# Moving the last sums of a frequency group behind the next group's first product in a fused Fourier filter and MLP

## The chip, the cores and the metric

The kernel runs on one core of a Trainium2 chip. The metric is the device time of one launch in microseconds. Names used below: TensorE (PE in the profile) multiplies matrices into PSUM; VectorE (DVE), ScalarE (ACT) and GpSimd (POOL) work elementwise; SyncE (SP) issues most transfers. Each engine takes its instructions in the order in which the program issues them, and waits where an operand is not ready.

## The reference

Two parts follow each other. A global Fourier filter along the sequence, and then a two-layer MLP whose activation is h - tanh(h):

```python
# batch 8, sequence 3008, channels 256, 1505 frequencies, d_ff 2048, all float32
X = np.fft.rfft(x, axis=1)
Y = X * (filt_r + 1j * filt_i)[None]
y = np.fft.irfft(Y, n=3008, axis=1)
t = y.reshape(8 * 3008, 256)
h = t @ w_in
out = (h - np.tanh(h)) @ w_out
```

## The kernel before

**Stages.** 3008 = 64 x 47, so the transform is made of matrix products. For each batch element b there are four stages. *First* (`first`): 12 steps of products of length 64, whose results go to a DRAM scratch tensor `ct1`. *Middle* (`middle`): products of length 47 forth, the multiplication with the filter, and products back, over seven groups of frequencies, from `ct1` to a second scratch tensor `ct2`. *Last* (`last`): products of length 64 back, from `ct2` into SBUF as the tokens of the MLP, in six chunks of four sequence rows. *MLP* (`up`, `shrink`, `down`): for every chunk, four quarters of d_ff.

**The loop.** The main loop runs over U, 4 quarters of 48 groups (8 elements b times 6 chunks c), 192 in all. At U it issues `up` of quarter U, `shrink` of U - 1 and `down` of U - 2, interleaved by hand inside `up` (L493 to L551). In `up` there are five slots, the calls `t(0)` to `t(4)`. A place in the loop is written (c, u, k) here: chunk, quarter, slot; its position in an element is 20c + 5u + k, from 0 to 119. While element p passes the MLP, the slots carry the middle stage of element p + 1 and the first stage of element p + 2 (for element 0, those of 1, and the first stages of 1 and 2). Element 7 has neither beside it.

**The order.** `planned` (L947) gives every step of these stages a due position: the 12 first steps and the 58 middle steps are each spread evenly from 0.2 to LAG (in element 0 the middle from LEAD = 30). `t(k)` (L994) takes the first step of the sorted list if its due position has come, one step for one slot. Slots 0 and 2 of quarter u = 3 are kept for `last` of the next chunk. A step is whatever a generator does up to its next `yield`.

**A middle group.** For group g of seven (six of 120 rows and one of 48) the steps are, with the names used below:

- F1: issue the loads of group g + 1 (`a2` from `ct1`, `ft`, the filter); two products (L327) into a PSUM bank, and ACT's copy to `xy` (L330).
- F2: two products (L327), and DVE's sum and difference with F1's result into `xy` (L332, L333).
- M1: POOL multiplies `xy` by the filter's real part into `nn` (L342, one buffer). M2: POOL multiplies `xy` by the imaginary part in place (L345).
- M3: POOL's two sums into `nn` (L347, L348).
- S: DVE's last sum and difference from `nn` into `xy` (L350, L351).
- B1 and B2: two products each (L361) from `xy`, ACT's copy (L364) and the write to `ct2` from ACT's queue.

`xy`, `a2`, `ft` and the copies `e1` have two buffers each. In the kernel before a group runs F1, F2, M1, M2, then B1 and B2 of the group before, M3, S.

**Banks.** The products of the slots go to a PSUM bank that `zd` chooses (L909): in slots 1, 2 and 3 it is bank `y` if the one before was `t`, otherwise `t`. Bank `y` is also the target of the second product of `up` in each quarter, which DVE reads at L509. So a product that a slot puts into `y` has to wait for L509 of its quarter. Bank `x` is freed for the next quarter by DVE's L534, bank `z` is read at L526 and L542.

**What DVE does in a quarter,** in program order: slot 0, L509, L564 (it waits for ACT's arctangent and square, L557 and L560), slot 1, L571 (it waits for ACT's square L568), slot 2, L526, L564, L534, slot 3, L571, slot 4, L542. (In element 0 slot 1 comes after the next product, and slot 3 before the last x product and L534.) Where u is 1, the sums of `down` come between (L632, L638, L643, L644, L650), and where u is 2 two transposes at slot 2 (L671). POOL forms four sums of the activations after the second L571 (`combine`, L466 to L469 on `t`), and four of the tokens after `last` (the same lines on `tu`).

Of the kernel before, what the change touches and what calls it, by code (L numbers as in the profile page):

```python
# [28 lines left out]
SLOTS = [(a, min(SG, NA - a)) for a in range(0, NA, SG)]  # L29
# [4 lines left out]
FACTORS = [(0.28138768672943115, 0.18210311233997345, 0.5012423992156982),  # L34
           (0.28138768672943115, -0.6558710336685181, 0.19358105957508087)]

LEAD, LAG = 30, 102

S, K = 0.6389930153911744, 0.3476472316053873
A, B = 0.18659689165196622, -0.6846325776203513  # L40
# [51 lines left out]
def kernel(  # L92
# [32 lines left out]
    def ways(g, back):  # L125

        if g < len(SLOTS) - 1:
            m = [mats[0:KM, (3 * back + k) * KM:(3 * back + k + 1) * KM] for k in range(3)]
            return m[0], m[0], m[1], m[2]
        at = 6 * KM + 4 * back * KL  # L130
        return [mats[0:KL, at + k * KL:at + (k + 1) * KL] for k in range(4)]
# [168 lines left out]
    def rows(t, b, g, first_block=0, n=4):  # L300

        a, s = SLOTS[g]
        return dram(t[b], (first_block * NA + a) * NH * DM,
                    [[DM, s * NH], [NA * NH * DM, n], [1, DM]])

    def load_a2(b, g, tag="a2", bufs=2):

        n = SLOTS[g][1] * NH
        t = tr.tile([KM, 4, DM], F32, tag=tag, bufs=bufs, name="a2")
        nc.sync.dma_start(t[0:n], rows(ct1, b, g))  # L310
        return t

    def load_ft(g):
        n = SLOTS[g][1] * NH
        t = tr.tile([KM, 4, DM], F32, tag="ft", bufs=2, name="ft")
        nc.sync.dma_start(t[0:n], dram(filt_d, g * KM * 4 * DM, [[4 * DM, n], [1, 4 * DM]]))
        return t

    def forth(g, at, z):

        n = SLOTS[g][1] * NH
        xy = tr.tile([KM, 4, DM], F32, tag="xy", bufs=2, name="xy")[0:n]
        way = ways(g, 0)
        for v in (1, 0):
            pa = z("pa", [128, 2, DM])[0:n]
            for k in range(2):
                nc.tensor.matmul(pa[:, k], way[2 * v + k], at[0:n, 2 * v + k],  # L327
                                 start=True, stop=True)
            if v:
                ACT.copy(xy[:, 2:4], pa)  # L330
                yield xy
        V.tensor_add(xy[:, 0:2], pa, xy[:, 2:4])  # L332
        V.tensor_sub(xy[:, 2:4], pa, xy[:, 2:4])  # L333
        yield

    def filtered(g, xy, ft, by, by2):

        n = SLOTS[g][1] * NH
        ab = xy.rearrange("p (x v) c -> p x v c", v=2)
        fv = ft[0:n].rearrange("p (x v) c -> p x v c", v=2)  # L340
        nn = tr.tile([KM, 4, DM], F32, tag="nn", bufs=1, name="nn")[0:n]
        by.tensor_mul(nn.rearrange("p (x v) c -> p x v c", v=2), ab,  # L342
                      fv[:, :, 0:1].to_broadcast([n, 2, 2, DM]))
        yield
        by.tensor_mul(ab, ab, fv[:, :, 1:2].to_broadcast([n, 2, 2, DM]))  # L345
        yield
        by2.tensor_sub(nn[:, 0:4:3], nn[:, 0:4:3], xy[:, 1:3])  # L347
        by2.tensor_add(nn[:, 1:3], nn[:, 1:3], xy[:, 0:4:3])  # L348
        yield
        V.tensor_add(xy[:, 0:2], nn[:, 0:2], nn[:, 2:4])  # L350
        V.tensor_sub(xy[:, 2:4], nn[:, 0:2], nn[:, 2:4])  # L351
        yield

    def back(b, g, xy, z):

        n = SLOTS[g][1] * NH
        way = ways(g, 1)
        for v in range(2):
            pe = z("pe", [128, 2, DM])[0:n]
            for k in range(2):  # L360
                nc.tensor.matmul(pe[:, k], way[2 * v + k], xy[:, 2 * v + k],  # L361
                                 start=True, stop=True)
            e1 = tr.tile([KM, 2, DM], F32, tag="e1", bufs=2, name="e1")[0:n]
            ACT.copy(e1, pe)  # L364
            ACT.dma_start(rows(ct2, b, g, 2 * v, 2), e1)
            yield

    def middle(b, z):

        a2, ft = {0: load_a2(b, 0)}, {0: load_ft(0)}  # L370
        waiting = iter(())
        yield
        for g in range(len(SLOTS)):
            if g + 1 < len(SLOTS):
                a2[g + 1], ft[g + 1] = load_a2(b, g + 1), load_ft(g + 1)
            there = forth(g, a2.pop(g), z)
            xy = next(there)
            yield
            next(there)
            yield  # L380
            done = filtered(g, xy, ft.pop(g), G, G)
            next(done)
            yield
            next(done)
            yield
            for _ in waiting:
                yield
            next(done)
            yield
            if g + 1 == len(SLOTS):  # L390
                yield
            for _ in done:
                yield
            waiting = back(b, g, xy, z)
        yield
        for _ in waiting:
            yield

    def filter_rows(g):

        a, s = SLOTS[g]
        for v, src in enumerate((filt_r.tensor, filt_i.tensor)):
            if g < len(SLOTS) - 1:
                yield v, 0, NH * s, dram(src, (a + 1) * DM, [[NQ * DM, NH], [DM, s], [1, DM]])
                for m, n in ((1, 16), (17, 7)):
                    yield 2 + v, m * s, n * s, dram(src, (NQ * m - a - 1) * DM,
                                                    [[NQ * DM, n], [-DM, s], [1, DM]])
            else:
                yield v, 0, NH, dram(src, (a + 1) * DM, [[NQ * DM, NH], [1, DM]])
                yield v, NH, NH, dram(src, 0, [[NQ * DM, NH], [1, DM]])  # L410
                for m, n in ((1, 16), (17, 7)):
                    yield 2 + v, m, n, dram(src, (NQ * m - a - 1) * DM, [[NQ * DM, n], [1, DM]])
# [377 lines left out]
    with tc.tile_pool(name="tr", bufs=2) as tr, tc.manual_schedule():  # L790
        with tc.tile_pool(name="pro", bufs=1) as pro, \
# [79 lines left out]
            waiting = iter(())  # L871
            last_g = len(SLOTS) - 1
            for g in range(last_g + 1):
# [3 lines left out]
                xy = next(there)  # L877
# [3 lines left out]
                done = filtered(g, xy, fts.pop(g), V, G)  # L881
# [5 lines left out]
                waiting = back(0, g, xy, z0)  # L887
# [16 lines left out]
        with tc.tile_pool(name="dn", bufs=2) as dn, \  # L904
# [42 lines left out]
            def planned(p):  # L947

                def spread(n, lo, hi, *what):
                    return [(lo + (hi - lo) * k / n, *what, k) for k in range(n)]  # L950

                n_m = 8 * len(SLOTS) + 2
                f = [spread(NX, *((0.2, LEAD / 2) if b == 1 else (LEAD / 2, LEAD) if b == 2
                                  else (0.2, LAG)), firsts, b, first)
                     for b in ([1, 2] if p == 0 else [p + 2]) if b < BATCH]
                m = [spread(n_m, LEAD if p == 0 else 0.2, LAG, mids, b, middle)
                     for b in [p + 1] if b < BATCH]
                return sorted(sum(f + m, []), key=lambda s: s[0])

            firsts, mids = {1: fs}, {}  # L960
            for U in range(total + 2):
                i, u = divmod(U, 4)
                if U < total:
                    p, c = groups[i]
                    if c == 0 and u == 0:
                        steps = planned(p)
                    if u == 0 and i + 1 < len(groups) and c + 1 < NC:
                        e2s[i + 1] = load_e2(*groups[i + 1])
                    if u == 2 and i + 1 < len(groups) and c + 1 == NC:
                        assert not steps  # L970
                        e2s[i + 1] = load_e2(*groups[i + 1])
                    if u == 1 and c + 1 == NC:
                        for gens, ahead, what in ((mids, 2, middle), (firsts, 3, first)):
                            if p + ahead < BATCH:
                                gens[p + ahead] = what(p + ahead, z1)
                                next(gens[p + ahead])
                    if u == 2 and i + 1 < len(groups):
                        lasts = last(i + 1, z1)
# [91 lines left out]
```

## Time and profile before

| | us |
|---|---|
| median of three runs | 2903.82 (2903.04 to 2906.41) |
| the profiled execution | 2905.42 |
| its span | 2903.6 |
| TensorE busy | 2730.1 (94%) |
| VectorE busy | 2067.3 (71%) |
| GpSimd busy | 1897.8 (65%) |
| ScalarE busy | 1762.8 (61%) |
| mean granted TensorE clock | 0.977 |

Busy time of TensorE is the union of matrix instructions with modelled ends, so it also counts time at a lower clock. One product of 128 x 128 by 128 x 256 leaves two records; four records start 0.86 us apart from the next four when nothing waits. The first 145 us prepare the weights and the first element's transforms; the loop over U begins there. The waits in the profile are named by what came last: "PE pa L327 <- DVE h L509" is a product of F1 or F2 that waited for DVE's reading of bank y.

### The profile page before, as it was taken

The numbers are of one execution on the slowest core, as the hardware profiler recorded it, in microseconds if no ns is written. First come the engines' busy times: TensorE is split into PE (matmuls) and PEld (weight loads), VectorE is DVE, ScalarE is ACT, GpSimd is POOL, SyncE is SP. The second block draws the span as 40 slices with busy tenths as digits, with TensorE's granted clock in tenths as the row PEclk, the third lists the DMA queues.
The fourth block names the chain that finished last, engine by engine and source line by source line (L and its number), as shares of the span: only waits on it lengthen the run. The fifth ranks groups of instructions, "written<-read, shape, count | busy, mean of one in ns | idle before, by whom it ended". The sixth has DMA issues, their size and how long they took to land.

```text
span 2903.6 us, 36938 instructions
## 1 busy us (share of the span) xinstructions
PE 2730.1 (94%) x12830; PEld 2376.1 (82%) x12830; DVE 2067.3 (71%) x2283; ACT 1762.8 (61%) x2583; POOL 1897.8 (65%) x1391
## 2 busy tenths in 40 slices
PE   4499999999999999999999999999999999999998
PEld 3388888888888888898888888888888888799886
DVE  4777777777677767777677766767767777677776
ACT  2156566566665666566665666656666566566665
POOL 4557886767657776666666766576675777655553
PEclk7699999999999999999999999999999999999999
DMA  9474223223232332233223331232323122101010
GB/s 244 133 227 126 63 49 86 76 63 80 66 73 68 84 85 60 64 77 95 55 60 69 98 84 49 55 99 73 78 50 71 47 57 58 28 20 36 19 26 17
DMA packets 341639, 215.48 MB, mean 74 GB/s; under 512 B 227736, under 2 KB 300988, under 8 KB 341251
## 3 DMA queue, kind: packets, MB, share of 16 engines
q1 hardware_dynamic: 296851, 154.15, 22.7%
q10 hardware_dynamic: 39504, 50.61, 5.6%
q0 software_dynamic: 5088, 8.28, 1.1%
q8 instruction: 103, 1.69, 0.3%
q14 instruction: 93, 0.76, 0.1%
HBM read 137.83 MB, written 78.12 MB: 74 GB/s over the span
## 4 chain that ended last, share of the span: by engine, by line
PE 65%; DVE 13%; POOL 11%; issue 4%; ACT 3%; DMA 2%; SPq 0%; ACTq 0%; DVEq 0%; POOLq 0%
PE o L618 26%; PE x L486 17%; PE z L486 8%; PE y L486 4%; DVE h L564 4%; PE pu L452 3%; PE pe L361 3%; DVE h L571 2%; PE pa L327 2%; PE pf L295 2%; POOL nn L347 2%; POOL nn L348 2%; ACT y L560 2%; POOL t L469 2%; DVE xy L351 1%
## 5 line engine op out<-in xcount | busy, mean ns | idle before, releaser
L564 DVE TENSOR_TENSOR h<-h,y 128x1024 f32<-128x1024 f32 (+1 forms) x384 | 598.1, 1558 | 288.0 <-ACT y L560 287.4
L618 PE MATMUL o<-t,wd 128*128 128x256 f32 (+1 forms) x3072 | 776.0, 375 | 0.0
L571 DVE SCALAR_TENSOR_TENSOR h<-sq,h 128x1024 f32<-128x1024 f32 (+1 forms) x384 | 600.8, 1564 | 123.2 <-ACT sq L568 115.1
L618 PEld LDWEIGHTS o<-t,wd 128*128 128x128 f32 x3072 | 583.6, 190 | 69.6 <-issue 2.4
L466 POOL TENSOR_TENSOR t<-h 128x512 f32<-128x512 f32 (+1 forms) x190 | 240.7, 1267 | 604.1 <-DVE h L571 371.2
L486 PE MATMUL x<-tu,wu 128*128 128x256 f32 (+1 forms) x2304 | 593.4, 381 | 0.0
L618 PE MATMUL o<-h,wd 128*128 128x256 f32 (+1 forms) x2304 | 584.8, 376 | 5.4 <-DVE h L571 5.1
L486 PEld LDWEIGHTS x<-tu,wu 128*128 128x128 f32 x2304 | 439.6, 193 | 58.9 <-issue 5.6
L618 PEld LDWEIGHTS o<-h,wd 128*128 128x128 f32 x2304 | 432.7, 190 | 60.9 <-DVE h L571 11.3
L568 ACT ACTIVATE sq<-y,near_b 128x1024 f32<-128x1024 f32 (+1 forms) x384 | 435.1, 1133 | 25.8 <-DVE h L571 20.1
L557 ACT ACTIVATE y<-h 128x1024 f32<-128x1024 f32 (+1 forms) x384 | 397.4, 1035 | 12.4 <-ACT e L364 7.3
L560 ACT ACTIVATE y<-y 128x1024 f32<-128x1024 f32 (+1 forms) x384 | 399.7, 1041 | 6.5 <-ACT a L296 0.4
L492 ACT COPY s<-x 128x512 f32<-128x512 f32 (+1 forms) x192 | 110.8, 577 | 424.6 <-PE x L486 419.3
L492 ACT COPY u<-x 128x512 f32<-128x512 f32 (+1 forms) x384 | 221.0, 576 | 225.5 <-PE x L486 203.1
L469 POOL TENSOR_TENSOR t<-t,h 128x512 f32<-128x512 f32 (+1 forms) x190 | 351.9, 1852 | 0.0
L467 POOL TENSOR_TENSOR t<-h,t 128x512 f32<-128x512 f32 (+1 forms) x190 | 245.9, 1294 | 14.9
L468 POOL TENSOR_TENSOR t<-h 128x512 f32<-128x512 f32 (+1 forms) x190 | 244.8, 1288 | 0.0
L486 PE MATMUL x<-ut,wu 128*128 128x256 f32 (+1 forms) x768 | 199.7, 382 | 30.6 <-DVE h L534 29.7
L526 DVE TENSOR_TENSOR h<-z,u 128x512 f32<-128x512 f32 (+1 forms) x192 | 128.8, 671 | 104.8 <-ACT u L492 103.7
L486 PE MATMUL z<-tu,wu 128*128 128x256 f32 (+1 forms) x768 | 196.7, 379 | 3.4 <-DVE h L542 3.4
L486 PE MATMUL z<-ut,wu 128*128 128x256 f32 (+1 forms) x768 | 194.4, 375 | 1.1 <-DVE h L526 1.0
L486 PEld LDWEIGHTS x<-ut,wu 128*128 128x128 f32 x768 | 140.0, 189 | 67.7 <-DVE h L534 52.7
(116 smaller groups left out, 3469.5 us busy)
## 6 DMA issues: line engine op xcount, KB each, us to landing
e<-ct SPq DMA_DIRECT2D x48, 512.0 KB, 4.6
a<-ct SPq DMA_DIRECT2D x48, 480.0 KB, 5.0
ct<-e ACTq DMA_DIRECT2D x96, 240.0 KB, 2.6
ct<-a ACTq DMA_DIRECT2D x84, 256.0 KB, 3.0
x_sb<-in_x_dram SPq DMA_DIRECT2D x161, 128.0 KB, 4.2
ft<-filt SPq DMA_DIRECT2D x42, 480.0 KB, 6.6
out_dram<-ot SPq DMA_DIRECT2D x1248, 16.0 KB, 1.5
gt<-g SPq DMA_DIRECT2D x48, 256.0 KB, 3.1
```

What stands on the lines that cost most here:

```text
L466: by.tensor_sub(t[0], b[0][1], b[0][0])
L467: by.tensor_sub(t[1], b[1][1], t[0])
L468: by.tensor_sub(t[2], b[1][1], b[0][1])
L469: by.tensor_sub(t[3], t[1], b[1][0])
L486: nc.tensor.matmul(bank[:, k], wu[:, q - 1, (2 * u + k) * 128:(2 * u + k + 1) * 128], rhs[q - 1], start=(first and k == 0), stop=True, ski ...
L492: ACT.copy(t, X)
L557: ACT.activation(y[k], ht[k], AF.Arctan, scale=S)
L560: ACT.activation(y[k], y[k], AF.Square, accum_out=y_sums[:, 2 * U + k // 2:2 * U + k // 2 + 1])
L564: V.tensor_mul(ht[k], ht[k], y[k])
L568: ACT.activation(sq[k], y[k], AF.Square, bias=near_b, scale=A)
L571: V.scalar_tensor_tensor(out=ht[k], in0=sq[k], scalar=K, in1=ht[k], op0=ALU.add, op1=ALU.mult)
L618: nc.tensor.matmul(product(q), wd[:, q - 1, (2 * u + k) * 128: (2 * u + k + 1) * 128], rhs[q - 1][:, k], start=(u == 0 and k == 0 and q == ...
```

## The change

S of a group moves into the next group, behind that group's F1. F2 and M1 follow; then come B1 of the group before, M2, B2 of the group before, and M3. A group now runs F1, S of the group before, F2, M1, B1 of the group before, M2, B2 of the group before, M3. The number of steps stays 58. At the end of an element there are two empty steps, and then S, B1 and B2 of the seventh group. Before, there was one empty step, S, another empty step, B1 and B2. LAG is 104 in place of 102. `filtered`, `forth`, `back`, `planned` and the slots are as they were.

```diff
-LEAD, LAG = 30, 102
+LEAD, LAG = 30, 104
 ...
-        waiting = iter(())
+        before = None
         yield
         for g in range(len(SLOTS)):
             if g + 1 < len(SLOTS):
                 a2[g + 1], ft[g + 1] = load_a2(b, g + 1), load_ft(g + 1)
             there = forth(g, a2.pop(g), z)
             xy = next(there)
             yield
+            if before:
+                next(before[0])
+                yield
             next(there)
             yield
             done = filtered(g, xy, ft.pop(g), G, G)
             next(done)
             yield
-            next(done)
-            yield
-            for _ in waiting:
+            if before:
+                next(before[1])
                 yield
             next(done)
             yield
-            if g + 1 == len(SLOTS):
+            if before:
+                next(before[1])
                 yield
-            for _ in done:
-                yield
-            waiting = back(b, g, xy, z)
-        yield
-        for _ in waiting:
-            yield
+            next(done)
+            yield
+            before = done, back(b, g, xy, z)
+        yield
+        for k in (0, 1, 1):
+            yield
+            next(before[k])
+        yield
```

## The prediction

> **What bounds the kernel now.** First the page's first part and its chain: TensorE is busy 94% of the span, and 65% of the chain that ended last is its matmuls. But 13% is DVE and 11% POOL, among them the two filter sums on POOL (L347, L348) and a last sum (L351).
>
> ```profile
> PE 2730.1 (94%) x12830; PEld 2376.1 (82%) x12830; DVE 2067.3 (71%) x2283; ACT 1762.8 (61%) x2583; POOL 1897.8 (65%) x1391
> ...
> PE 65%; DVE 13%; POOL 11%; issue 4%; ACT 3%; DMA 2%; SPq 0%; ACTq 0%; DVEq 0%; POOLq 0%
> PE o L618 26%; PE x L486 17%; PE z L486 8%; PE y L486 4%; DVE h L564 4%; PE pu L452 3%; PE pe L361 3%; DVE h L571 2%; PE pa L327 2%; PE pf L295 2%; POOL nn L347 2%; POOL nn L348 2%; ACT y L560 2%; POOL t L469 2%; DVE xy L351 1%
> ```
>
> Next the windows, one for each batch element. Element 2 (of 0 to 7, a middle stage beside it) leaves TensorE 11.1 us idle of 348.2, element 6 12.4 of 341.1, element 7, with no middle stage beside it, 0.6 of 283.8:
>
> ```profile
> 846.90:1195.10 348.20, 337.11 (x1602) 295.12 (x1602) 246.03 (x263) 219.39 (x321) 232.00 (x161) 0.99 0.30 74
> ...
> 2239.90:2581.00 341.10, 328.73 (x1554) 286.59 (x1553) 253.71 (x263) 212.44 (x309) 241.02 (x161) 0.98 0.20 48
> 2581.00:2864.80 283.80, 283.18 (x1369) 252.51 (x1368) 208.37 (x226) 191.18 (x275) 162.47 (x124) 1.00 0.11 24
> ```
>
> The waits name the pair: DVE stands 106.3 us in front of the last sums, and TensorE waits for DVE sums that are queued behind them.
>
> ```profile
> DVE xy L350 <- POOL nn L348: 106.3, 35, 6.6
> ...
> PE pa L327 <- DVE h L509: 40.0, 11, 5.0
> ...
> PE x L486 <- DVE h L534: 29.7, 39, 1.5
> ```
>
> The timeline of element 1 shows how, first DVE, then PE. S.0 sits at slot (0,2,0) (chunk, quarter, slot). It waits for POOL until 529.07; L509, which frees bank y, is behind it; F1.1 at the next slot wants bank y, so TensorE stands from 527.8 to 532.8.
>
> ```profile
> 529.07 1.60 DVE L350 TENSOR_TENSOR xy<-nn 120x512 f32<-120x512 f32 x1 [2.21 <-POOL nn L348]
> 530.60 1.61 DVE L351 TENSOR_TENSOR xy<-nn 120x512 f32<-120x512 f32 x1
> 532.13 0.61 DVE L509 TENSOR_TENSOR h<-y,s 128x448 f32<-128x448 f32 x1
> ```
>
> ```profile
> 526.05 1.78 PE L618 MATMUL o<-h,wd 128*128 128x224 f32 x8
> 532.80 1.84 PE L327 MATMUL pa<-a,mats_sb 120*120 120x256 f32 x4 [4.96 <-DVE h L509]
> ```
>
> Afterwards the granted clock is half (column PEclk, third from the end, 0.50), so the stall of 5.1 costs 6.9:
>
> ```profile
> 533.10:536.40 3.30, 3.30 (x10) 2.77 (x9) 1.05 (x1) 0.82 (x2) 2.73 (x3) 0.50 0.00 0
> ```
>
> The Trainium skill ("TensorE: Matmul & The Clock Gate", Part 1) has the clock fall after an idle window of about 3.4 us. Here it also fell after stalls of 2.65 us (0.50 at 623 to 625 us), so by the page those five stalls would have cost 1.7 us less each; the trace decides.
>
> **What is at stake.** I take the starts of successive y products as the length of a quarter. In element 7 a quarter is 12.09 us (12.41 where u is 1, 13.87 where u is 3, near 11.5 in chunk 0), 24 of them 297.7. A product of four records adds 4 x 0.216 = 0.86. Elements 1 to 5 carry 28 middle and 12 first products more: 297.7 + 40 x 0.86 = 332.2, measured 348.2, so 16.0 lost in each. Where: (0,2) 19.46 against 12.59, 6.9; (2,0) 19.11 against 14.68, 4.4; (3,1) 15.41 against 14.14, 1.3; (4,2) 1.3; (4,0) 1.0; the rest 1.1. Element 6: 341.1 - 321.9 = 19.2, mostly (4,0) 6.7 and (0,2) 5.4. Element 0, by the same differences from (1,3) on: 10.6. In all 10.6 + 5 x 16.0 + 19.2 = 110 us.
>
> **The change, part by part.** Nothing is added to or taken from any engine; instructions move. I laid out both orders on the slots by the rule in the code (one step in each free slot whose place has come; a slot is 348.2 / 120 = 2.9 us).
>
> *LAG 104.* The spacing grows from 101.8 / 58 = 1.755 to 103.8 / 58 = 1.790 slots. The last back product moves from place 100.2 to 102.2; the next element's e2 load stands at 110, over 20 us later, and the write lands in 2.6 us. Cost nothing; without that cover, the load's 4.6 us once per element.
>
> *S one step later, behind F1.* S.0 goes to (0,2,1), F1.1 in front of it. L509 no longer stands behind S, so F1.1 starts at once. By the rows POOL is through at 529.04, and DVE comes to S about 529.6 (the ACT squares ended 527.73; F1's copy 0.59 and L564 1.2 come first), so no wait. The pair costs 3.2 beside POOL's L466 (1.60 and 1.61, against 0.69 alone), leaving L534 0.4 late for bank x and F2's sums 0.6 late for bank y: 1.1 instead of 6.9.
>
> At (2,0) it is not cured: M3.2 falls at (1,3,4), one slot later than now, which puts it behind the four L466 to L469 sums on POOL. Now it runs in front of them:
>
> ```profile
> 614.16 2.25 POOL L348 TENSOR_TENSOR nn<-nn,xy 120x512 f32<-120x512 f32 x1
> 616.37 1.27 POOL L466 TENSOR_TENSOR t<-h 128x512 f32<-128x512 f32 x1
> ```
>
> L571 ends near 615.7, four sums of 1.27 to 1.7 reach 621, M3 2.5 to 4.5 more: 624.5. S.2 at (2,0,1) ends about 626; then end sum 1.2, F2's pair 1.4, L526 0.7, L564 1.2, L534 0.7: 631.2. TensorE wants bank z at 627.9 (L526 ends 629.3) and bank x at 630.2: 1.4 + 1.0 = 2.4, range 0.5 to 5. F2.3 itself on y isn't held, since L509 is ahead of S. Now it costs 4.4.
>
> The other S: at (1,1,1) and (2,3,1) M3 is four and five slots old, no wait; at (3,1,4) and (4,0,3) S stands behind L534 and delays only L542 and L509, which have slack; at (5,0,0) the back product follows at the next slot: TensorE needs 0.86 + 0.86 + 1.73 from bank z's last product, DVE 0.68 + 1.35 + 0.68, taken as 0.5. So (3,1) goes from 1.3 to about 0 with 0.2 at (3,2), (4,0) from 1.0 to 0.2.
>
> The present loss at (3,1): the 3.63 us in front of L350 push L534, which frees bank x:
>
> ```profile
> 699.98 0.69 DVE L350 TENSOR_TENSOR xy<-nn 120x512 f32<-120x512 f32 x1 [3.63 <-POOL nn L348]
> ...
> 705.18 0.68 DVE L534 COPY h<-x 128x512 f32<-128x512 f32 x1
> ```
>
> *Back products behind M1 and M2.* S lies three steps (15 us) ahead of them, no cost. Alternating with steps that use no bank, they mostly get another bank; twice an element (at (0,3), (3,3)) two products in t follow each other over slots 3 and 4, each perhaps 0.3 for ACT's copy (0.58): 0.6. M3.6 goes from slot 2 of (4,2), beside the transposes L671, to slot 4: 1.3 to about 0.6.
>
> *Queues and buffers.* M1 needs the single nn buffer two steps after S instead of three; at (2,0) S ends 626, M1.3 comes after 629: nothing. F1's loads on SP's queue now stand three steps behind M2 of the group before, not five; SP already waits 163.8 us for M2 (20 times), in front of stores of 1.5 us and loads used eight steps (40 us) later, landing in 6.6: nothing. ACT's ct2 writes follow their products; POOL's queue holds no DMA here after 323 us.
>
> *Sum.* Elements 1 to 5: 1.1 at (0,2), 2.4 at (2,0), 0.5 at (5,0), 0.4 for (3,2) and (4,0), 0.6 for bank t, 0.6 at (4,2) and 0.9 of the present rest = 6.5 for 16.0, 5 x -9.5 = -47.5. Element 6: S.0 and S.5 at (0,2,1) and (4,0,3), no late S left but (2,0,0): about 5 for 19.2, -14. Element 0: S.2 and S.4 come to slot 0 with F2 on y at slot 1, but there the sums of L466 on ut are through before; 8 for 10.6, -2.6. Together -64. Against it stands one price that the slots don't settle: the pair of S takes 1.4 on a free DVE, 3.3 beside POOL, now 2.0 in the mean (L350 944 ns, L351 1053). Over 49 moved pairs that is 29 us less to 64 more, and by the 2.7 us that two sums late at L534 cost at (2,1) of element 0 it can reach TensorE in full. I take the middle, +17, as POOL is busy for 65% of the span. So -47.
>
> The Trainium skill ("SBUF — State Buffer", "SBUF: two separate sides") calls that an exclusive lock: a DVE instruction with two SBUF inputs waits out the POOL instruction. The rows agree (L350 ended 0.55 us after POOL's L466 did, at 530.12). Were S to meet M1 or M2 (3.2 us each), the rule would make the pair 6.4, which is 2.9 above what the slower rival takes; no S does so by the slots.
>
> The profiled execution took 2905.42 (span 2903.6); 2905.4 - 47 = 2858. The median of the three runs, 2903.82, is 1.6 below, inside what I can resolve.
>
> **The rivals.** *Half of it (0.18).* Only the big stalls of 5.4 to 6.9 go (5 x 5.8 + 4.5 + 6.3 = 40), and (2,0) gets a cold clock, 5 x 1.7 back: 2874. For it: M3.2 behind the combine. Against: the waits in five other quarters end as surely.
>
> *Everything hidden (0.10).* The full 110 goes: 2796; 80 of it, 2826. For it: DVE is only 71% busy. Against: (2,0).
>
> *Slower: DVE in front of L534 (0.12).* S and F2's sums now stand in neighbouring steps. If both fall ahead of L534 in one quarter, S at its longest row (1.75 each), DVE is 3.5 + 1.4 = 4.9 late, less what it idles there (1.1 in front of L571, 1.0 in front of L526): 2.8 for each of 49 groups against 110 / 49 = 2.2 now, +27: 2932. It decides above 2.2 a group. For it: DVE's idle time is spread and S has no cover of its own. Against: only at (2,0) do both stand there; F2 falls behind L534 in three other groups.
>
> *No change (0.05).* Each wait is paid at the next bank: 2903, within 6 us (0.2%, about what three runs from 2903.0 to 2906.4 can tell).
>
> **How the numbers follow.** Forecast 0.55 with its own range 2838 to 2876 (the residue of 6.5 down to 3 or up to 10 in each element). Faster 0.55 + 0.18 + 0.10 = 0.83, same 0.05, slower 0.12. The range 2826 to 2896 leaves out the slower case, no change, and the far end of the hidden one.
>
> **What would show it.** Right: the wait of pa on L509 from 40 us to under 10; DVE's wait for L348 from 106 to under 40, what is left at (2,0); no half clock after (0,2); elements near 339. Wrong: pa or pe waiting for L350 or L509 at new slots, x waiting for L534 over 40 us, half-clock stretches more than five.

## The result, and the profile after

Median of four runs 2877.05 us (2872.96 to 2878.8), against 2903.66 (2903.04 to 2906.41) for four of the kernel before: ratio 0.9904, 95% interval 0.9887 to 0.9922. The change is faster by 26.6 us where 47 was forecast. The time lies inside the range on record (2826 to 2896) and 1 us outside the forecast's own (2838 to 2876); of the cases, "Half of it" with 2874 came nearest. The profiled execution took 2878.8, its span is 2877.0, the mean granted clock 0.982 (before 0.977).

The page of the kernel after, its first and its fourth part (busy time, and the chain that ended last). From L368 on, line numbers are five higher than before: L514 is the old L509, L539 the old L534.

```profile
PE 2719.1 (95%) x12830; PEld 2361.4 (82%) x12830; DVE 2105.3 (73%) x2283; ACT 1761.2 (61%) x2583; POOL 1927.1 (67%) x1391
...
PE 68%; DVE 17%; POOL 4%; issue 4%; ACT 4%; DMA 3%; SPq 1%; ACTq 0%; DVEq 0%; POOLq 0%
```

POOL's share of the chain fell from 11% to 4%: it is no longer waited for in the old place. DVE's rose from 13% to 17%, and DVE is busy for 38 us more though it executes the same 2283 instructions. The windows of elements 2 and 6 (length, then busy time by engine, clock and DMA) show the gain and its limit: 348.2 became 343.0, and of that TensorE is still idle for 7.8; 341.1 became 334.0.

```profile
847.10:1190.10 343.00, 335.18 (x1602) 292.15 (x1601) 253.44 (x263) 219.23 (x321) 237.67 (x161) 1.00 0.31 75
2219.10:2553.10 334.00, 326.65 (x1554) 284.26 (x1553) 258.24 (x263) 212.32 (x309) 244.43 (x161) 0.99 0.21 49
```

The waits of DVE and of TensorE after (who waits for what: us in total, times, longest):

```profile
DVE xy L350 <- POOL nn L348: 29.4, 16, 4.5
```

```profile
PE x L491 <- DVE h L539: 26.9, 37, 4.1
...
PE pa L327 <- DVE h L514: 10.3, 7, 1.7
...
PE o L623 <- POOL t L473: 6.2, 8, 0.9
...
PE pe L361 <- DVE h L514: 5.0, 5, 1.0
```

DVE's wait in front of the last sums went from 106.3 to 29.4. Seven of the 16 that remain lie ahead of the loop (20.3 us; a kernel below keeps these alone), and only 6.4 of the rest at (2,0). TensorE's wait for the reading of bank y went from 40.0 to 10.3. New are a wait of `o` for POOL's combining, and one of B's products (`pe`) for bank y.

The place that the prediction showed, S.0 of an element (here element 2), first DVE, then TensorE. F1.1 starts at 874.52 with no wait in front of it, S.0 has its operands, and the clock in the stretch that was cold before is full (1.00; before, at 881.40 to 884.70, it was 0.51).

```profile
879.71 1.62 DVE L350 TENSOR_TENSOR xy<-nn 120x512 f32<-120x512 f32 x1
881.25 1.62 DVE L351 TENSOR_TENSOR xy<-nn 120x512 f32<-120x512 f32 x1
```

```profile
874.52 1.03 PE L327 MATMUL pa<-a,mats_sb 120*120 120x256 f32 x4
...
882.37 1.40 PE L623 MATMUL o<-t,wd 128*128 128x224 f32 x6 [0.89 <-POOL t L473]
```

The trace's clock record has 13 stretches at half clock from the loop's start to the end of element 6 before, and 3 after. Two of the three are new, in element 0 and in element 6, both at (2,1). In element 0 S stands 1.59 us for M3 in front of L539, and x behind it for 4.12, so the stall that the change takes from (0,2) has come back there in front of another bank. The last section comes to the one in element 6.

```profile
294.05 0.69 DVE L350 TENSOR_TENSOR xy<-nn 120x512 f32<-120x512 f32 x1 [1.59 <-POOL nn L348]
294.66 1.72 DVE L351 TENSOR_TENSOR xy<-nn 120x512 f32<-120x512 f32 x1
296.31 0.68 DVE L539 COPY h<-x 128x512 f32<-128x512 f32 x1
```

```profile
297.04 2.08 PE L491 MATMUL x<-ut,wu 128*128 128x256 f32 x4 [4.12 <-DVE h L539]
```

Lengths of the elements, from the starts of the y products, in us:

| element | 0 | 1 | 2 | 3 | 4 | 5 | 6 | rest |
|---|---|---|---|---|---|---|---|---|
| before | 353.2 | 348.6 | 348.2 | 348.2 | 348.2 | 348.4 | 341.1 | 322.7 |
| after | 358.6 | 343.0 | 343.0 | 343.0 | 343.0 | 343.0 | 334.0 | 324.0 |

Where the code of an element is unchanged, its length still differs by 2 to 4 us from kernel to kernel (the rest from 320.0 to 324.0), so only larger differences of a single element are read below. In elements 1 to 5 of the kernel after, the same quarter has the same length within 0.1 us. A quarter's length also holds its slots' products, 0.86 us each; where an edit moves one into another quarter, the text says so.

### The profile page after: what moved, and what is told of

The parts are those of the page before. It is cut to its first block, busy times and chain, and to the rows that moved or that the text cites. A ratio compares the mean times of both kernels' runs of the same rounds, so it can differ in the third digit from the quotient of the medians.

```text
span 2877.0 us, 36939 instructions
## 1 busy us (share of the span) xinstructions
PE 2719.1 (95%) x12830; PEld 2361.4 (82%) x12830; DVE 2105.3 (73%) x2283; ACT 1761.2 (61%) x2583; POOL 1927.1 (67%) x1391
## 4 chain that ended last, share of the span: by engine, by line
PE 68%; DVE 17%; POOL 4%; issue 4%; ACT 4%; DMA 3%; SPq 1%; ACTq 0%; DVEq 0%; POOLq 0%
PE o L623 28%; PE x L491 17%; PE z L491 8%; PE y L491 5%; DVE h L569 5%; DVE h L576 3%; PE pu L457 3%; PE pe L361 3%; PE pa L327 2%; PE pf L295 2%; DVE xy L351 2%; ACT y L565 1%; DMA x<-in_x_dram 1%; DVE h L539 1%; POOL nn L348 1%
## 5 line engine op out<-in xcount | busy, mean ns | idle before, releaser
L569 DVE TENSOR_TENSOR h<-h,y 128x1024 f32<-128x1024 f32 (+1 forms) x384 | 604.2, 1574 | 274.4 <-ACT y L565 274.2
L576 DVE SCALAR_TENSOR_TENSOR h<-sq,h 128x1024 f32<-128x1024 f32 (+1 forms) x384 | 614.8, 1601 | 104.3 <-ACT sq L573 95.3
L471 POOL TENSOR_TENSOR t<-h 128x512 f32<-128x512 f32 (+1 forms) x190 | 239.1, 1258 | 587.4 <-DVE h L576 345.6
L491 PE MATMUL x<-tu,wu 128*128 128x256 f32 (+1 forms) x2304 | 583.7, 376 | 1.5 <-ACT u L497 1.5
L491 PEld LDWEIGHTS x<-tu,wu 128*128 128x128 f32 x2304 | 432.1, 190 | 57.2 <-issue 5.2
L474 POOL TENSOR_TENSOR t<-t,h 128x512 f32<-128x512 f32 (+1 forms) x190 | 318.1, 1674 | 0.0
L473 POOL TENSOR_TENSOR t<-h 128x512 f32<-128x512 f32 (+1 forms) x190 | 267.7, 1409 | 0.0
L491 PE MATMUL x<-ut,wu 128*128 128x256 f32 (+1 forms) x768 | 203.1, 387 | 27.9 <-DVE h L539 26.9
L514 DVE TENSOR_TENSOR h<-y,s 128x512 f32<-128x512 f32 (+1 forms) x192 | 129.9, 676 | 93.7 <-PE y L491 84.3
L491 PE MATMUL y<-ut,wu 128*128 128x256 f32 (+1 forms) x768 | 195.8, 378 | 2.6 <-DVE xy L333 2.6
```

Of the source, the lines that this page charges most:

```text
L471: by.tensor_sub(t[0], b[0][1], b[0][0])
L473: by.tensor_sub(t[2], b[1][1], b[0][1])
L474: by.tensor_sub(t[3], t[1], b[1][0])
L491: nc.tensor.matmul(bank[:, k], wu[:, q - 1, (2 * u + k) * 128:(2 * u + k + 1) * 128], rhs[q - 1], start=(first and k == 0), stop=True, ski ...
L569: V.tensor_mul(ht[k], ht[k], y[k])
L576: V.scalar_tensor_tensor(out=ht[k], in0=sq[k], scalar=K, in1=ht[k], op0=ALU.add, op1=ALU.mult)
```

## The experiments

All ratios are against the kernel before, run on the same chip, with 95% intervals. The theory at the start was the prediction's: S and what is queued behind it on DVE is the cost, and what is left of the gain is S beside POOL's adding.

### Which part of the change does it

**LAG alone.** The kernel before with

```diff
-LEAD, LAG = 30, 102
+LEAD, LAG = 30, 104
```

> The kernel before with LAG = 104 and nothing else. Theory S (the gain is S no longer standing, unfinished by POOL, ahead of the read of bank y): S.0 is still at slot (0,2,0) with F1.1 on bank y behind it and S.2 comes to (2,0,0) straight behind M3.2, so both big stalls stay: 2895 to 2915 us. Rival LAG (the wider spacing of the steps alone made the gain): about 2877 us.

Measured: 2911.43 us, 1.0021 [1.0011, 1.0031]. Spreading the steps wider gives nothing, it costs 6 us. Quarter (0,2) of element 2 is longer than before (20.92), (2,0) shorter (15.68), and (2,1) goes from 13.82 to 16.52, as in the changed kernel; one product of 0.86 has moved from (2,0) to (2,1). So the second of the two big stalls did shrink, from a loss of 4.4 to 1.9, which the expectation did not have, and the first one grew.

**The way back alone.** The kernel before with LAG 104, B1 behind M1 and B2 behind M2, S where it was:

```diff
             next(done)
             yield
-            next(done)
-            yield
-            for _ in waiting:
+            if g:
+                next(waiting)
+                yield
+            next(done)
+            yield
+            if g:
+                next(waiting)
                 yield
```

> Only B1 and B2 are moved (B1 behind M1, B2 behind M2); S stays the step behind M3, LAG = 104. Theory S: S.0 at (0,2,0) ahead of F1.1 on bank y, as before: 2895 to 2915. Rival B: 2870 to 2885.

Measured: 2910.09 us, 1.0018 [1.0009, 1.0028]. No gain. TensorE's waits in these two, of the first and of the second kernel, still have the old culprit (L513 there is the old L509):

```profile
PE pa L327 <- DVE h L509: 37.7, 13, 5.0
```

```profile
PE pa L327 <- DVE h L513: 38.1, 13, 5.0
```

**S alone.** The changed kernel with B1 and B2 together behind M2:

```diff
-            if before:
-                next(before[1])
-                yield
             next(done)
             yield
             if before:
                 next(before[1])
                 yield
+                next(before[1])
+                yield
```

> Only S is moved behind the next F1; B1 and B2 stay together behind M2, LAG = 104. Theory S: the same as the changed kernel within 8 us, 2869 to 2885. Rival B (the gain comes from parting B1 and B2, which gives each its own bank): 2895 to 2910.

Measured: 2890.3 us, 0.9948 [0.9932, 0.9965]. Faster by 15, where S alone was to give 20 or more; the rival's range was missed by as much on the other side. So S is the part that gains, and B1 and B2 apart, worth nothing alone, give 13 more on top of it. In element 2 the difference is 2.0 us: TensorE's waits for x fall from 4.4 (7 times) to 3.2 (5 times), those of B's products for bank y from 1.3 to 1.0. Why the parting works only together with S was not tested.

**The new order with the old spacing.** The changed kernel with LAG = 102.

> The changed kernel with LAG = 102. Theory S: the stall at (0,2) stays away (S.0 at slot (0,2,1)), while S.2 comes to (2,0,0) with F2.3 on bank y at the next slot, so some 3 to 4 us an element come back there: 2875 to 2895 us. Rival LAG: about 2904 us.

Measured: 2874.9 us, 0.9896 [0.9874, 0.9918]: the same as after. The losses change places: (2,1), (3,2) and (5,0) of element 2 become 13.82, 13.82 and 14.46 (after: 16.53, 16.59, 15.54; the first two with one product fewer), while (2,0), (4,2), (3,1) and (1,1) become 17.66, 15.17, 14.92 and 14.62 (after: 14.74, 12.96, 13.28, 13.07; (3,1) with one more). The place that the theory named is there: at (2,0) F2.3 stands 1.90 us for L514, the granted clock is half behind it in elements 2 to 5, and the quarter loses 3.9.

```profile
959.71 1.99 PE L327 MATMUL pa<-a,mats_sb 120*120 120x256 f32 x4 [1.90 <-DVE h L514]
```

```profile
960.00:963.00 3.00, 3.00 (x8) 2.33 (x8) 2.49 (x3) 0.00 (x0) 2.39 (x2) 0.50 0.31 74
```

Elements 2 to 5 are 1.7 to 2.1 us longer for it (344.7 to 345.1 instead of 343.0), and element 0 is 4.9 shorter (353.7 instead of 358.6).

### What S costs in either order

**No S, new order.** S is left out in elements 1 to 7, so the last sums are not computed and B's products take what M2 left in `xy`:

```diff
+        if by is not G:
-        V.tensor_add(xy[:, 0:2], nn[:, 0:2], nn[:, 2:4])
-        V.tensor_sub(xy[:, 2:4], nn[:, 0:2], nn[:, 2:4])
+            V.tensor_add(xy[:, 0:2], nn[:, 0:2], nn[:, 2:4])
+            V.tensor_sub(xy[:, 2:4], nn[:, 0:2], nn[:, 2:4])
```

> The changed kernel with S left out in elements 1 to 7 (the last sums aren't computed, B1 and B2 take what M2 left in xy; all else is kept). Theory residue: each element from 343.0 to about 338 (1.9 at (3,2), 1.1 at (5,0), about 2 at (0,2) go), element 0 some 8 less: 2840, between 2830 and 2855. If what is left is POOL's M products holding DVE, (2,1) and (1,2) keep their 1.5 and 1.2.

Measured: 2836.22 us, 0.9759 [0.9742, 0.9775], as expected.

**No S, old order.** The same edit in the kernel before.

> The kernel before with S left out in elements 1 to 7, in the same way. Theory S (where S stands is nearly all of the difference between the two kernels): within 8 us of the changed kernel without S, 2832 to 2855. Rival (parting B1 and B2 and the wider spacing carry 13 us of it): 13 or more slower than the changed kernel without S.

Measured: 2826.47 us, 0.972 [0.9704, 0.9736]. Not within 8 us of the other: the old order without S is 10 us the faster one. This is the most telling pair of the study. In the old order S costs 1 - 0.972 of 2905, 81 us; in the new one 0.9904 - 0.9759, 42. So the change takes 39 us off the price of S, and its other moves, LAG among them, cost 11: 28 together. With those moves at nothing the gain would have been 39; for 47, another 8 would have had to come off the 42 that S still costs.

By element, S costs 10.7 to 11.5 us in elements 1 to 5, 13.6 in element 6 and 8.3 in element 0 in the old order, and 5.0 to 5.3, 4.2 and 12.2 in the new one. In element 0 the new order does not make S cheaper.

The quarters of element 2 say where the 5.3 us that S still costs there lie, changed kernel against the one without S: (3,2) 16.59 and 14.69, (5,0) 15.54 and 14.46, (2,0) 14.74 and 13.82, (0,2) 15.89 and 14.98, (2,1) 16.53 and 16.05. The sum of the differences is 5.3. Three quarters stay long without any S: (0,2), (2,1), (1,2).

### Where the rest of S's price lies

The timeline of the changed kernel at (3,2) of element 2, DVE and then PE. S.4 runs at slot (3,1,4) beside POOL's four combining sums and takes 3.5 us, L547 and L514 are queued behind it, and F2.5, on bank y, waits for L514.

```profile
1048.33 1.72 DVE L350 TENSOR_TENSOR xy<-nn 120x512 f32<-120x512 f32 x1
1049.97 1.76 DVE L351 TENSOR_TENSOR xy<-nn 120x512 f32<-120x512 f32 x1
1051.65 0.68 DVE L547 TENSOR_TENSOR h<-z,u 128x512 f32<-128x512 f32 x1
1052.25 0.68 DVE L514 TENSOR_TENSOR h<-y,s 128x512 f32<-128x512 f32 x1
```

```profile
1052.98 1.12 PE L327 MATMUL pa<-a,mats_sb 120*120 120x256 f32 x4 [1.40 <-DVE h L514]
```

**S held back from slots 4 and 0.** The changed kernel, where S of groups 0 to 5 waits for another slot if it would come to slot 4 or 0, and S of group 6 stands two steps ahead of its B1 (this second part is not printed):

```diff
-                    elif steps and steps[0][0] <= pos:
+                    elif steps and steps[0][0] <= pos and not (
+                            p and steps[0][3] is middle and k in (0, 4)
+                            and steps[0][4] in (6, 14, 22, 30, 38, 46)):
```

> The changed kernel, but in elements 1 to 7's middle stages that run beside the MLP of elements 1 to 6, S of groups 0 to 5 is held back while the slot is 4 or 0 (straight ahead of L514), and S of group 6 goes two steps ahead of B1. Theory residue: (3,2) from 16.6 to about 15 and (5,0) from 15.5 to 14.9, so some 2.3 us an element and 13 in all: 2864, between 2856 and 2872. Rival (the stall moves to the next bank again): 2872 to 2885.

Measured: 2867.34 us, 0.987 [0.9854, 0.9886]. As expected: an element goes from 343.0 to 340.8, (3,2) from 16.59 to 14.14, (5,0) from 15.54 to 14.91, with a product that moves to (4,0) (13.28 to 14.23).

**And the old order beside element 0.** The kernel above, in which the middle stage beside element 0 runs in the order and with the LAG of the kernel before (`middle_old`, not printed):

```diff
-                m = [spread(n_m, LEAD if p == 0 else 0.2, LAG, mids, b, middle)
+                m = [spread(n_m, LEAD if p == 0 else 0.2, LAG if p else 102, mids, b,
+                            middle if p else middle_old)
```

> The kernel that holds S back from slots 4 and 0, and beside element 0 alone also the old order of the middle stage's slots with the old lead of 102 groups, in which S, B1 and B2 stand together behind M2. Theory that element 0's price is the new order's: element 0 goes from 357.0 back to about 353 us (353.2 in the kernel before), the others stay at 340.8 to 340.9: 2862 us (2855 to 2868). Rival, that the later start of element 0's own groups sets it: no gain, 2867.

Measured: 2866.64 us, 0.9863 [0.9846, 0.988]. No gain beyond the one before. Element 0 came back from 357.0 to 354.8, no more than the scatter between kernels, and element 6 and the rest, unchanged in their code, were 4.6 longer together. Whether the old order helps element 0 is not settled.

**S on POOL, new order.** The changed kernel, in elements 1 to 7:

```diff
-        V.tensor_add(xy[:, 0:2], nn[:, 0:2], nn[:, 2:4])
-        V.tensor_sub(xy[:, 2:4], nn[:, 0:2], nn[:, 2:4])
+        by3 = G if by2 is G and by is G else V
+        by3.tensor_add(xy[:, 0:2], nn[:, 0:2], nn[:, 2:4])
+        by3.tensor_sub(xy[:, 2:4], nn[:, 0:2], nn[:, 2:4])
```

> The changed kernel with S computed by POOL in place of DVE, in elements 1 to 7. DVE loses 1.4 to 3.5 us a group and POOL gains 2.5 to 4.5. Theory residue (what the changed kernel still loses at (0,2), (3,2) and (5,0) is S's pair on DVE ahead of L514, L531 and L539): 2840 to 2868. Rival POOL (the late POOL sums that TensorE waits for, 6.2 us on t L473, are the next bound): 2877 or slower, to 2900.

Measured: 2907.99 us, 1.0001 [0.9992, 1.0011]. The whole gain is lost, but not as the rival had it. TensorE's waits name one new place:

```profile
PE pe L362 <- POOL xy L351: 35.7, 9, 5.2
```

It is (5,0), 20.33 us instead of 15.54, where B1.6 comes right behind S.6 (seven of the nine waits), and (2,0) and (4,0) of element 0 (369.5). The other quarters are as without S: (2,0) 13.82, (0,2) 14.98.

### What the other moves cost

**No M2.** The changed kernel, where POOL in elements 1 to 7 doesn't multiply by the imaginary half of the filter; `xy` keeps what F2 wrote:

```diff
-        by.tensor_mul(ab, ab, fv[:, :, 1:2].to_broadcast([n, 2, 2, DM]))
+        if by is not G:
+            by.tensor_mul(ab, ab, fv[:, :, 1:2].to_broadcast([n, 2, 2, DM]))
```

> The changed kernel with M2 left out in elements 1 to 7 (POOL doesn't multiply by the imaginary half of the filter; its tile keeps what F2 wrote, so this part of the filter is not computed). Theory that POOL's products hold VectorE's activations of the next chunk, which TensorE's x product waits for: (2,1) goes from 16.5 to about 15.0 us, (1,2) from 14.1 to about 13.0, and M3 ends 3 us sooner; 3 to 5 us an element, 2850 to 2865 us in all. Rival, that these quarters are long by their extra products and VectorE's own work alone: they stay, about 2877 us.

Measured: 10148.22 us in all, 3.4922 [3.4864, 3.498], which says nothing on M2. After the loop the program tests the arguments of its activation, and where they are out of bounds it computes the MLP once more by a general branch; without M2 they were, and that branch took 7.3 ms. The loop ahead of it can be read. An element has 339.9 us instead of 343.0, and element 6 ends at 2530.0 us after the start instead of 2553.0. These 23 us, taken off 2877, give 2854, inside the theory's 2850 to 2865. (2,1) went from 16.53 to 14.75 as the theory had it, (0,2) from 15.89 to 14.83, which it hadn't; (1,2), where 13.0 was expected, stayed at 14.11.

The timeline at (2,1) of element 2 shows the mechanism. First POOL and DVE of the changed kernel, M1.3 and M2.3 beside L569 and L576:

```profile
980.10 2.36 POOL L342 TENSOR_TENSOR nn<-xy,ft 120x1024 f32<-120x1024 f32 x1
982.54 3.22 POOL L345 TENSOR_TENSOR xy<-xy,ft 120x1024 f32<-120x1024 f32 x1
```

```profile
980.61 2.93 DVE L569 TENSOR_TENSOR h<-h,y 128x1024 f32<-128x1024 f32 x1
983.64 3.20 DVE L576 SCALAR_TENSOR_TENSOR h<-sq,h 128x1024 f32<-128x1024 f32 x1
```

Then DVE at the same place without M2 (one line further, L570 and L577):

```profile
973.83 2.93 DVE L570 TENSOR_TENSOR h<-h,y 128x1024 f32<-128x1024 f32 x1
976.86 1.23 DVE L577 SCALAR_TENSOR_TENSOR h<-sq,h 128x1024 f32<-128x1024 f32 x1
```

L576 takes 1.23 us alone and 3.20 beside M2; L569, which still meets M1, keeps its 2.93. Each of the held ones ends 1.08 us after POOL's product does (983.54 after 982.46, 986.84 after 985.76), so it does nearly all of its work once POOL is through. The Trainium skill ("SBUF — State Buffer", "SBUF: two separate sides") describes an exclusive lock between such a DVE instruction, with two SBUF inputs, and one of GpSimd; the rows agree. x then waits for L539, further on in DVE's order: 1.4 us, the longest wait of x in this element.

With LAG 104, (2,1) has 16.5 us in either order (16.52 with LAG alone, 16.51 with B alone), and with 102 it has 13.82 in either (before, and the new order with 102): it is the spacing that puts M2.3 there (and one product of 0.86, part of the difference). M2 meets DVE's instructions in the kernel before too, elsewhere; what it costs there was not measured.

### A version that beats both

**S of groups 0 to 5 on POOL, of group 6 on DVE,** in the kernel with the old order beside element 0:

```diff
-            done = filtered(g, xy, ft.pop(g), G, G)
+            done = filtered(g, xy, ft.pop(g), G, G, G if g < 6 else V)
```

(the sixth argument is the engine of S; the lines of `filtered` that use it are not printed)

> As the one before, and S of groups 0 to 5 is done by POOL in elements from the second on; S of group 6 stays with VectorE, since B1 of that group comes right behind it. Theory that what is left of S is the pair on VectorE beside POOL's adding: quarter (0,2) goes from 15.9 to 15.0 us, (2,0) from 14.7 to 13.8, two or three microseconds an element: 2848 to 2858 us. Rival, that POOL's added 2.5 us a group make its other results late: 2870 us or more, with TensorE waiting for POOL at M3's or the combining's readers.

Measured: 2847.61 us, 0.9797 [0.978, 0.9814]. As expected: (0,2) 14.99, (2,0) 13.82, an element 338.4 to 339.6.

**The same edit in the kernel before,** with its own order and LAG 102, nothing moved.

> The kernel before, in its own order and with its own lead, in which POOL does S of groups 0 to 5 right behind its M3; S of group 6 stays with VectorE. Theory that the order before was only bad because VectorE, queued, waited for M3, and is otherwise the better one by some 10 us: elements of 337 to 340 us instead of 348.2, nearly the 336.7 of the order before without S, and 2830 to 2850 us. Rival, that S's 2.5 us on POOL make the combining behind it late for TensorE's output products in (0,2) and (2,0): elements of 342 to 345, 2855 to 2880 us, with TensorE's wait for L469 up from under 1 to 2 or 3 us at each of them.

Measured: 2846.32 us (2843.57 to 2851.07), 0.9802 [0.9786, 0.9819]: 31 us faster than the change, equal to the one above, with four changed lines in `filtered` and its call in place of the whole reordering. Its elements 1 to 5 have 337.7 to 338.9 us, one or two more than with no S at all (336.7 to 337.9); (0,2) has 14.58 instead of 19.46, (2,0) 14.68 instead of 19.11. The rival's late combining is there, but small. TensorE's waits of this kernel, and DVE's:

```profile
PE x L486 <- DVE h L534: 23.7, 36, 1.3
...
PE o L618 <- POOL t L468: 10.0, 13, 1.5
...
PE o L618 <- POOL t L466: 4.4, 7, 1.3
```

```profile
DVE xy L350 <- POOL nn L348: 20.3, 7, 4.5
```

No product waits for bank y behind S any more, and the seven waits of DVE for M3 are those ahead of the loop. The groups of this kernel, by line (busy time, mean ns, idle before), show that the gain isn't a lighter DVE:

```profile
L564 DVE TENSOR_TENSOR h<-h,y 128x1024 f32<-128x1024 f32 (+1 forms) x384 | 640.9, 1669 | 309.3 <-ACT y L560 308.6
L571 DVE SCALAR_TENSOR_TENSOR h<-sq,h 128x1024 f32<-128x1024 f32 (+1 forms) x384 | 629.3, 1639 | 99.8 <-ACT sq L568 91.7
...
L351 POOL TENSOR_TENSOR xy<-nn 120x512 f32<-120x512 f32 x42 | 80.8, 1924 | 0.0
L350 POOL TENSOR_TENSOR xy<-nn 120x512 f32<-120x512 f32 x42 | 65.5, 1559 | 1.5
```

S left DVE (111.9 us of L350 and L351 before, 21.7 now), but L564 and L571 have 1270.2 together where they had 1198.9 before, held by the POOL sums. DVE is busy for 2057.6 us instead of 2067.3, nearly as long. What went is its waiting, in order, for another engine.

## Why the prediction was right, and where it was not

**The mechanism was right.** S standing on DVE in front of M3, with L509 queued behind it, was the large stall; moving S behind F1 took it away, and neither LAG nor the parting of B did so alone. Of the signs, DVE's wait for L348 came under 40 as stated (29.4, though most of it ahead of the loop and not at (2,0)), and the full clock after (0,2); x's wait (26.9) and three half-clock stretches stayed below what would have been wrong (40 and five). pa's wait for bank y just missed (10.3, stated under 10). One sign of "wrong" came: pa and pe wait for L514 at new slots; and elements are 343.0, not near 339.

**The sum was too large.** Its terms against what the traces have:

| term | forecast | measured |
|---|---|---|
| elements 1 to 5 | -47.5 | -26.6 |
| element 6 | -14 | -7.1 |
| element 0 from (1,3) | -2.6 | +4.8 |
| start, element 0 before (1,3), element 7 and end | 0 | +2.3 |
| sum | -64 | -26.6 |
| held against it, S beside POOL | +17 | |
| forecast | -47 | |

In elements 1 to 5 the residue was put at 6.5 us and is 10.8 (16.0 before). By its steps, losses as the prediction counts them:

- *(0,2), 1.1 forecast, 3.3 measured.* The sums behind S were counted, POOL's queue was not. TensorE's `o` waits 0.89 for L473 (and z, x and y for 1.5 together), and the old stall had covered that. Without S 2.4 of it stays, and without M2 1.06 goes.
- *(2,0), 2.4 forecast, 0.9 measured.* M3.2 did fall behind the combining, as laid out, but POOL was through sooner: S.2 stood on DVE for 1.16 and started at 967.69, and only x was late. This rests on LAG 104: with 102 the quarter loses 3.9, with the cold clock.
- *(3,2), 0.2 forecast, 1.9 measured.* The step that failed is "at (3,1,4) and (4,0,3) S stands behind L534 and delays only L542 and L509, which have slack". At (4,0) the loss is 0.3. At (3,1,4) it had none: S took 3.5 us beside the combining, and F2.5 at the next free slot was on bank y and waited 1.40.
- *(5,0), 0.5 forecast, 1.7 measured.* B1.6 behind S.6 was seen, but with the pair at 1.35; beside POOL it took 1.47 and 1.75, and pe waits 1.0 for L514.
- *(2,1) 1.5 and (1,2) 1.2, nothing forecast.* "Cost nothing", said of LAG 104, looked at the last step's room at the element's end alone. The spacing also decides beside which DVE instruction POOL's 3.2 us products run, and at (2,1) M1.3 and M2.3 met L569 and L576. At (1,2) M1.2 and M2.2 stand beside the same two instructions (2.23 and 2.76 us); without M2 the quarter stays, so what holds it is not settled.
- *The rest.* (4,0) has 0.3 as put down, (4,2) none; for (4,2), bank t and the present rest 2.1 were forecast and nothing measurable is left. The seven measured losses add up to the 10.8.

*Element 0.* "there the sums of L466 on ut are through before" overlooked the four sums on `t`: S takes 3.5 us beside them at (3,0) and at (4,0), and F2 on bank y waits 1.7 for L514 in each. That (2,1) there has 19.10 instead of 16.81, with S standing in front of L539 and x waiting 4.1, was not foreseen.

**The +17 held against it.** As a time of DVE it was nearly exact: L350 and L351 rose from 111.9 to 128.1 us, 16 more. But it was one mean price for S alone. DVE's L569 and L576 are lengthened in the same way, and POOL's products, moved by the same change, were left out of the account: without M2 an element of the new order is 3.1 us shorter. How much of this the kernel before pays too is open.

**The rivals.** "Half of it" gave nearly the right time by another way, which is luck: it wanted a cold clock at (2,0), and there is none (with LAG 102 there is, at the same total time). "Everything hidden" needed S at no price; with S gone altogether the new order only reaches 2836. "DVE in front of L534" (2932) did not come as a whole: x's wait fell from 29.7 to 26.9, though (2,1) of element 0 shows such a place. As for the clock, the stalls at (2,0) that the prediction puts at 2.65 us are 2.49 in the profile's idle time; with LAG 102 one of 1.90 is followed by the half clock too.

## What to carry to other kernels

Where an engine stands, in order, in front of another engine's result, first ask whether the waiting instruction can move to the engine that makes the result. There it is in order and waits for nothing: here moving two sums to POOL did more (59 us) than moving steps (27 us). It holds where no product of TensorE comes right behind the moved step: at (5,0), with S.6 on POOL, the quarter grew from 15.54 to 20.33. Before an order is changed, take the suspected step out in the old and in the new order: the two times price the step in each order, and the rest of the reordering. And when a step is moved, lay out every long POOL instruction of the new order against the two-input DVE instructions that it will meet; the free slots of TensorE don't show that.

## What the hardware showed that was not expected

- DVE instructions that were not part of the change were lengthened by where POOL's products fell: 1.23 to 3.20 us (L576 beside M2).
- The price is mutual. S on POOL has a mean of 1559 and 1924 ns for sums that take 1.26 us where nothing meets them (shortest row of L350 on POOL, 1259 ns), and DVE's L564 and L571 grew by 71 us in all. TensorE's wait for x, which L534 behind L564 frees, did not grow with it (23.7 us, 29.7 before).
- Stalls of about 2 us were enough for the half clock, as one or as two close together. With LAG 102 a single one of 1.90 us at (2,0) is followed by 0.50 in elements 2 to 5; in element 1 the clock stays at 1.00 behind 1.89, and in element 0 of the changed kernel behind 1.68 and 1.72. In (2,1) of element 6 of the changed kernel TensorE stands 0.78 us in front of z and, one group of products later, 1.39 in front of x; then the granted clock is 0.52:

```profile
2355.55 1.13 PE L491 MATMUL z<-ut,wu 128*128 128x256 f32 x4 [0.78 <-DVE h L531]
2358.07 1.73 PE L491 MATMUL x<-ut,wu 128*128 128x256 f32 x4 [1.39 <-DVE h L539]
```

```profile
2359.00:2362.00 3.00, 3.00 (x8) 2.37 (x8) 1.44 (x4) 2.13 (x3) 2.63 (x3) 0.52 0.02 5
```

  In elements 1 to 5 the same quarter has the wait of x alone, and the clock stays at 1.00. The Trainium skill ("TensorE: Matmul & The Clock Gate", "Part 1: The HAM clock gate") speaks of an idle window of about 3.4 us; neither of these stalls is that long, nor are both together, nor is the one of 1.90.
- Losses came back in other places, to the same total, when only the spacing changed (2877.05 with LAG 104, 2874.9 with 102, intervals 0.9887 to 0.9922 and 0.9874 to 0.9918), though twelve quarters of element 2 differ by 0.3 to 2.9 us (in some of them by a product of 0.86).
